# Moving half of a K slot to the front of the load queue, ahead of two weight matrices

## The chip, the cores and the metric

The kernel runs on one core of one Trainium2 chip. The metric is device time in microseconds (us), the median of several executions. The profile's span is some 1.4 us shorter than the device time of the same execution, so spans are compared with spans and times with times.

## The reference

Two decode attention blocks with one query token each, A and B, are computed and their outputs joined. Both have 32 query heads, 16 key/value heads of 128, and a cache of 8192 positions. A looks only at the last 2048 of them, B at all.

```python
q = (x @ wq).reshape(B, Sq, 32, 128)              # x: 1 x 576, wq: 576 x 4096
scores = einsum("bhqd,bhkd->bhqk", q, k) * 128 ** -0.5
o = einsum("bhqk,bhkd->bhqd", softmax(scores), v)
out = o.reshape(B, Sq, 4096) @ wo                 # wo: 4096 x 576
# A: k, v = the last 2048 positions of the cache;  B: all 8192
return concatenate([a, b], axis=-1)
```

Almost all of the work is to read the caches and weights once: 102.76 MB.

## The kernel before

One large tensor, `slots`, holds 4 x 16,384 elements per partition. Slots 0 and 1 take K, slots 2 and 3 take V. Five rounds go through it: round 0 for A, rounds 1 to 4 for B. At the start, parts of it lend their place to the two query weights, `wq`:

```python
SLOT, WQ_W = 16384, 18432
...
WQ = [(4 * SLOT - WQ_W, [("v", 2)]),                           # A's wq: end of the V slots
      (SLOT, [("k", 1, 0), ("k", 1, 1), ("v", 0)])]            # B's wq: K slot 1 and a little of V
for P in range(2):
    off, res = WQ[P]
    x_columns(P)
    load(slots[:, off:off + WQ_W], ... wqs[P] ..., res, "wq%d" % P)   # 128 runs of 36 KB
    q_part(P, off, res)                                        # 36 products that read this wq
    q_finish(P)
...
for g in range(NG):
    for s in range(2):
        load_k(g, s)
    load_v(g)
    ...
```

All these loads are issued by SyncE, in program order, on one queue that the 16 transfer engines serve. A helper derives the waits from `reads` and `writes`: a load waits until the last reader of its place is done. So the load of K slot 1 for A (issued in line 411 of the kernel before) waits for the 36 products on B's wq. A's two K slots are loaded in halves of 2 MB:

```python
for m1 in range(2):                                            # in load_k, for g == 0
    i = 8 * m1 + s
    src = ks[0][0, i:i + 7:2, SK - W_A:, :].rearrange("h (p t) d -> p h (t d)", t=64)
    ins = sp.dma_start(dst[:, m1 * 2 * UNIT:(m1 + 1) * 2 * UNIT], src)   # 128 runs of 16 KB
```

The very first load of the program is issued ahead of the block's opening barrier. The loads are thus issued in this order: A's wq, B's wq, two halves of A's K slot 0, (wait), two halves of A's K slot 1, V.

## Time and profile before

| | before |
|---|---|
| device time, median of 3 | 245.37 us (245.37 to 245.59) |
| span of the profile | 244.0 us |
| bytes read | 102.76 MB |
| share of 16 engines' span taken by the main queue | 98.3% |
| busiest compute engine (TensorE) | 68% |

The kernel is bound by transfers; what counts is any time in which the transfer engines have nothing to do. In the view of busy time by stretch, the columns are the stretch and its length, the five compute engines, TensorE's granted clock, the mean share of the transfer engines in use, and GB/s.

```profile
33.00:34.50 1.50, 0.00 (x0) 0.00 (x0) 0.00 (x0) 0.00 (x0) 0.00 (x0) 0.50 0.95 404
34.50:44.00 9.50, 9.31 (x131) 8.11 (x132) 6.16 (x6) 6.85 (x7) 0.00 (x0) 0.83 1.01 429
```

The engines pass from slot 0 to slot 1 with 0.95 of them in use (transfers are counted by their starts, so values swing a little around 1).

### The profile page before, as it was taken

How to read it: one execution, taken by the hardware profiler on the slowest of the kernel's cores; microseconds unless marked ns; L12 is line 12 of the kernel's file. 1: busy time of each engine (PE TensorE's matmuls, PEld its weight loads, DVE VectorE, ACT ScalarE, POOL GpSimd, SP SyncE). 2: the span in 40 equal slices, each digit the busy share in tenths (PEclk: the TensorE clock that was granted, in tenths of full speed). 3: DMA queues.
4: the chain of work that ended last, by engine and by line, in shares of the span. 5: the costliest groups of instructions: out<-in, count | busy, mean ns of one | idle time of the engine just before them, and what ended most of it. 6: DMA issues, size and time to landing. Idle time of an engine off the chain costs nothing. (4 is left out here: it accounts for less than half of the span.)

```text
span 244.0 us, 5212 instructions
## 1 busy us (share of the span) xinstructions
PE 165.8 (68%) x2325; PEld 120.5 (49%) x2325; DVE 88.2 (36%) x152; ACT 93.2 (38%) x96; POOL 6.4 (3%) x33
## 2 busy tenths in 40 slices
PE   0007539958397997394999473999446699845964
PEld 0002238745237775243978231987332687535753
DVE  0001218855304555203465322456322165533030
ACT  2000018845303876301687500678600387630000
POOL 5000100000000000000000000000000000000000
PEclk9999959997867999657699959799958799965799
DMA  9999999999999999899999999999989999989994
GB/s 344 429 405 422 435 432 422 427 424 427 459 432 426 489 397 462 371 430 435 483 410 451 403 403 435 435 494 408 473 365 440 430 494 397 473 380 417 426 405 172
DMA packets 4064, 102.88 MB, mean 422 GB/s; under 512 B 596, under 2 KB 728, under 8 KB 984
## 3 DMA queue, kind: packets, MB, share of 16 engines
q1 hardware_dynamic: 3896, 102.76, 98.3%
q8 instruction: 6, 0.10, 0.2%
q10 hardware_dynamic: 160, 0.00, 0.0%
q14 instruction: 2, 0.02, 0.0%
HBM read 102.76 MB, written 0.00 MB: 421 GB/s over the span
## 5 line engine op out<-in xcount | busy, mean ns | idle before, releaser
L506 ACT ACTIVATE kt<-ktps 128x1024 bf16<-128x1024 bf16 x80 | 79.8, 1040 | 87.3 <-PE ktps L496 87.2
L496 PE MATMUL ktps<-ident,slots 128*128 128x128 bf16 x1280 | 87.9, 234 | 22.6 <-PEq L214 19.6
L496 PEld LDWEIGHTS ktps<-ident,slots 128*128 128x128 bf16 x1280 | 81.7, 106 | 38.5 <-issue 38.5
L509 DVE COPY kt<-ktps 128x1024 bf16<-128x1024 bf16 x80 | 60.7, 774 | 59.6 <-PE ktps L496 59.6
L588 PE MATMUL opsum<-slots,ptm 128*32 128x512 bf16 x320 | 27.4, 515 | 7.7 <-PEq L214 7.7
L521 PE MATMUL sacc<-kt,qst 128*32 128x512 bf16 x320 | 25.8, 398 | 2.3 <-PEq L214 2.3
L588 PEld LDWEIGHTS opsum<-slots,ptm 128*32 128x32 bf16 x320 | 13.3, 125 | 20.3 <-issue 18.0
L559 PE MATMUL misc<-ident,psb 128*128 128x128 bf16 x40 | 4.3, 271 | 15.8 <-PEq L214 15.8
L547 ACT ACTIVATE psb<-sacc,stat 128x2048 bf16<-128x2048 f32 x5 | 9.8, 1967 | 9.8 <-DVE stat L536 9.8
L606 DVE TENSOR_TENSOR vtmp<-opsum,maskV 128x512 f32<-128x512 f32 x4 | 2.8, 691 | 27.7 <-PE opsum L588 27.7
L438 PE MATMUL misc<-xnine,twice 64*128 64x18 bf16 x1 | 0.2, 170 | 17.8 <-DMA xnine<-in_B_x_dram 17.8
L559 PEld LDWEIGHTS misc<-ident,psb 128*128 128x128 bf16 x40 | 3.1, 118 | 18.3 <-issue 18.3
L521 PEld LDWEIGHTS sacc<-kt,qst 128*32 128x32 bf16 x320 | 5.0, 94 | 8.4 <-issue 4.9
L566 DVE TENSOR_TENSOR ptm<-misc,maskP 128x1024 bf16<-128x1024 bf16 x5 | 3.5, 692 | 15.6 <-PE misc L559 15.6
L438 PEld LDWEIGHTS misc<-xnine,twice 64*128 64x128 bf16 x1 | 0.1, 99 | 17.8 <-issue 17.8
L703 ACT ACTIVATE outsb<-ktps 64x144 bf16<-64x144 f32 x1 | 0.3, 288 | 21.1 <-PE ktps L691 21.1
L691 PE MATMUL ktps<-slots,opj 128*32 128x144 bf16 (+1 forms) x192 | 6.8, 247 | 2.2 <-DMA slots<-in_B_wo_dram 2.2
L462 ACT ACTIVATE qrow<-opsum 128x512 bf16<-128x512 f32 x1 | 0.6, 597 | 19.2 <-PE opsum L456 19.2
L691 PEld LDWEIGHTS ktps<-slots,opj 128*32 128x32 bf16 x192 | 5.2, 97 | 3.6 <-DMA slots<-in_B_wo_dram 3.0
L447 DVE TENSOR_SCALAR xpad<-misc,par 128x5 bf16<-128x5 f32 (+1 forms) x8 | 1.2, 228 | 13.6 <-PE misc L438 13.6
L481 POOL COPY qst<-qcol 128x32 bf16<-128x32 bf16 x8 | 1.7, 213 | 147.5 <-PE sacc L521 147.5
L559 PE MATMUL turned<-ident,psb 128*128 128x128 bf16 x40 | 5.3, 314 | 0.0
(76 smaller groups left out, 57.9 us busy)
## 6 DMA issues: line engine op xcount, KB each, us to landing
slots<-in_B_k_cache_dram SPq DMA_DIRECT2D x8, 4096.0 KB
slots<-in_A_k_cache_dram SPq DMA_DIRECT2D x4, 2048.0 KB
slots<-in_A_v_cache_dram SPq DMA_DIRECT2D x4, 2048.0 KB
slots<-in_A_wq_dram SPq DMA_DIRECT2D x1, 4608.0 KB, 13.9
slots<-in_B_wq_dram SPq DMA_DIRECT2D x1, 4608.0 KB, 24.0
slots<-in_A_wo_dram SPq DMA_DIRECT2D x1, 4608.0 KB, 19.8
slots<-in_B_wo_dram SPq DMA_DIRECT2D x1, 3024.0 KB, 26.6
slots<-in_B_wo_dram SPq DMA_DIRECT2D x1, 1008.0 KB, 9.2
```

Source lines behind the costliest of these rows:

```text
L447: add("dve", lambda dve, dst=dst, o=320 + 9 * P + i, n=n, e=e: dve.tensor_scalar(dst, misc[:, o:o + n], par2[:, e:e + 1], None, ALU.mult), ...
L481: return pool.tensor_copy(dst, src)
L496: ins = pe.matmul(ktps_bf[q][:, t * 128:(t + 1) * 128], lhsT=slots[:, o:o + 128], rhs=ident[:, :], start=True, stop=True, is_transpose=True)
L506: add("act", lambda act, src=src, dst=dst: act.activation(dst, src, ACT.Copy), reads=[("bank", q)], writes=[("kt", u % NKT, q)], tag="e%d% ...
L509: add("dve", lambda dve, src=src, dst=dst: dve.tensor_copy(dst, src), reads=[("bank", q)], writes=[("kt", u % NKT, q)], tag="e%d%d" % (u, q))
L521: ins = pe.matmul(sacc[32 * j:32 * j + 32, :], lhsT=qst[:, o:o + 32], rhs=rhs, start=(u == 0 and e == 0), stop=True, skip_group_check=True)
L547: return act.activation(dst, src, ACT.Exp, bias=st(C_NB + g), scale=SCALE, accum_out=st(C_L + g))
L559: ins = pe.matmul(dst[:, t * 128:(t + 1) * 128], lhsT=psb[:, o:o + 128], rhs=ident[:, :], start=True, stop=True, is_transpose=True)
L566: return dve.tensor_tensor(ptm[:, c * 1024:(c + 1) * 1024].rearrange("p (t y) -> p t y", t=8), dst.rearrange("p (t y) -> p t y", t=8), mas ...
L588: ins = pe.matmul(opsum[64 * j + 32 * x:64 * j + 32 * x + 32, :], lhsT=ptm[:, o:o + 32], rhs=v[:, at[0], at[1], :, :, b:b + 128], start=(n ...
L606: add("dve", lambda dve: dve.tensor_tensor(vtmp[:, :, :], src, by, ALU.mult), reads=[B_O, w], writes=["vtmp"], tag="keep")
L691: ins = pe.matmul(ktps[P + j // 2][32 * j:32 * j + 32, 0:w], lhsT=opj[:, P, at:at + 32], rhs=slots[:, o:o + w], start=(jj == 0), stop=(jj ...
```

## The change

The intent: let the very first transfer be one of short runs (16 KB in place of 36 KB). No byte is added; the first half of A's K slot 0 is taken out of its place behind both wq and put ahead of them.

```diff
-            for m1 in range(2):
-                i = 8 * m1 + s
-                src = ks[0][0, i:i + 7:2, SK - W_A:, :].rearrange("h (p t) d -> p h (t d)", t=64)
-                ins = sp.dma_start(dst[:, m1 * 2 * UNIT:(m1 + 1) * 2 * UNIT], src)
-                if m1 == 0:
-                    op.also.append((32, ins))
-            return ins
-        op = add("sp", go, writes=KS[s], dma="k%d" % s, inc=64)
+            if s == 0:
+                return half_of_A(sp, s, 1)
+            op.also.append((32, half_of_A(sp, s, 0)))
+            return half_of_A(sp, s, 1)
+        op = add("sp", go, writes=KS[s], dma="k%d" % s, inc=64 if g or s else 32)
+
+    def half_of_A(sp, s, m1):
+        ... the load of one half, as above ...
@@
     WQ = [...]
+
+    add("sp", lambda sp: half_of_A(sp, 0, 0), writes=["first"], dma="k0", inc=32)
     for P in range(2):
```

More of the change, by code (lines that the diff above doesn't have):

```diff
@@ L407, in go @@
                 return sp.dma_start(dst, ks[1][0, i:i + 3:2, :, :].rearrange("e (p t) d -> p e (t d)", t=128))
-            for m1 in range(2):
-                i = 8 * m1 + s
-                src = ks[0][0, i:i + 7:2, SK - W_A:, :].rearrange("h (p t) d -> p h (t d)", t=64)
-                ins = sp.dma_start(dst[:, m1 * 2 * UNIT:(m1 + 1) * 2 * UNIT], src)
-                if m1 == 0:
-                    op.also.append((32, ins))
-            return ins
-        op = add("sp", go, writes=KS[s], dma="k%d" % s, inc=64)
+            if s == 0:
[4 more added lines that the diff above has]
+    def half_of_A(sp, s, m1):
+        i = 8 * m1 + s
+        src = ks[0][0, i:i + 7:2, SK - W_A:, :].rearrange("h (p t) d -> p h (t d)", t=64)
+        return sp.dma_start(slots[:, koff(s) + m1 * 2 * UNIT:koff(s) + (m1 + 1) * 2 * UNIT], src)
     def load_v(g):
```

## The prediction

> **What bounds the kernel now.** I began with the page's rows over time and its queue table, to see which resource has no gaps.
>
> ```profile
> PE 165.8 (68%) x2325; PEld 120.5 (49%) x2325; DVE 88.2 (36%) x152; ACT 93.2 (38%) x96; POOL 6.4 (3%) x33
> ...
> DMA  9999999999999999899999999999989999989994
> GB/s 344 429 405 422 435 432 422 427 424 427 459 432 426 489 397 462 371 430 435 483 410 451 403 403 435 435 494 408 473 365 440 430 494 397 473 380 417 426 405 172
> ...
> q1 hardware_dynamic: 3896, 102.76, 98.3%
> ```
>
> No compute engine is above 68%. The transfer engines are at 9 tenths nearly everywhere, and SyncE's queue (q1) keeps all sixteen occupied for 98.3% of the span. Only the first slice (344 GB/s) and the last (172) are low. So time can be won or lost only where the queue stands empty: before the first byte, after the last, or in a hole in between.
>
> The chain that ended last, in order of time, agrees: it ends in a wait for the last weight transfer and a short tail of products and output.
>
> ```profile
> 231.52 0.33 SPq L398
> 231.85 0.04 issue
> 231.89 9.93 DMA slots<-in_B_wo_dram
> 241.82 0.04 issue
> 241.87 0.64 PE ktps L691 x16
> ```
>
> Then I asked for busy time by stretch, for the start, where the change lies. The last two columns are the mean share of the transfer engines in use and GB/s.
>
> ```profile
> 0.00:1.00 1.00, 0.00 (x0) 0.00 (x0) 0.00 (x0) 0.00 (x0) 0.41 (x6) 1.00 0.00 0
> 1.00:3.00 2.00, 0.00 (x0) 0.00 (x0) 0.00 (x0) 0.99 (x1) 2.00 (x8) 1.00 1.13 313
> 3.00:6.00 3.00, 0.00 (x0) 0.00 (x0) 0.46 (x2) 0.50 (x2) 1.19 (x6) 1.00 0.97 418
> 6.00:14.00 8.00, 0.00 (x0) 0.00 (x0) 0.00 (x0) 0.00 (x0) 0.00 (x0) 1.00 1.01 433
> ```
>
> One microsecond passes before any byte. The trace's records of single packets (one packet is one contiguous run) say more: the first packet of an engine starts at 1.04 to 1.5 us (one engine at 2.3), and takes a median of about 2.2 us, where every later 36 KB packet takes 1.364 us. So each engine pays about 0.85 us once for a cold start. That 0.85 us is all that a different first packet could save, since the microsecond before it comes from issuing at all.
>
> The timeline of the issuing queue and of the first weight products gives the dependences of the start:
>
> ```profile
> 0.00 0.41 SPq L398 DMA_DIRECT2D slots<-in_A_wq_dram  x1
> 0.80 0.35 SPq L398 DMA_DIRECT2D slots<-in_B_wq_dram  x1
> ...
> 17.84 0.17 PE L438 MATMUL misc<-xnine,twice 64*128 64x18 bf16 x1 [17.84 <-DMA xnine<-in_B_x_dram]
> ...
> 18.82 4.03 PE L456 MATMUL opsum<-slots,xpad 128*32 128x512 bf16 x36 [0.81 <-DVE xpad L447]
> ...
> 24.80 3.40 PE L456 MATMUL turned<-slots,xpad 128*32 128x512 bf16 x36 [0.99 <-DMA slots<-in_B_wq_dram]
> ```
>
> A narrower window of the same view shows the issue of A's second K slot,
>
> ```profile
> 28.24 1.20 SPq L411 DMA_DIRECT2D slots<-in_A_k_cache_dram  x2
> ```
>
> and the waits of the issuing queue name what holds it up:
>
> ```profile
> SPq L411 <- PE turned L456: 25.7, 1, 25.7
> ```
>
> B's wq lies in the second K slot, so A's second K slot may be issued only when the 36 products that read B's wq are done (28.2 us). Until then the transfer engines live on what was queued before, ending with A's first K slot. By the packet records, the sixteen engines finish that slot between 33.0 and 34.1 us. The queue thus has 33.0 - 28.2 = 4.8 us of **reserve**, less about 1.05 us from issue to first byte. That is the number to watch.
>
> **What the Trainium skill says.** "DMA: Bandwidth & Descriptors", section "Where 436 GB/s comes from", puts the ceiling of 16 ports at 435.2 GB/s. The trace agrees: 16 x 36,864 bytes / 1.364 us = 432 GB/s, and 428 GB/s for 16 KB packets (0.612 us). Run length is therefore worth 1% and the change alters no run's length, only the order. The same page, "Queues, rings and completion order", says that each engine serves its queues in turn, packet by packet. The trace agrees: x, 18-byte packets on ScalarE's queue, passes between packets of wq one at a time and lands 11.4 and 16.4 us after issue. "Perfetto Trace Analysis", "DMA Instruction — HWDGE (DVE, Sync)", says that the slice of a transfer instruction does not contain its data movement; here a slice of 0.41 us stands for a wq that lands after 13.9 us, so I time transfers by packets and by waits. "TensorE: Matmul & The Clock Gate", Part 1, says that the array runs at half clock after an idle window of about 3.4 us and needs as much sustained work to speed up. The trace agrees: the first 36 products advance four per 0.43 us throughout (4.03 us), while the second 36, begun only 0.99 us after other work, speed up in their last groups (3.40 us).
>
> **The change part by part.** Bytes, packets and instruction kinds stay; the instruction order shows one of the four half-slot loads moved ahead of both wq, and nothing else.
>
> (a) *First packets of 16 KB in place of 36 KB.* If the 0.85 us is the latency of a first read that nothing hides, it does not depend on size and nothing is won. If part of it grows with the packet, at most 0.85 us is. I take a gain of 0.2 us.
>
> (b) *x lands earlier.* Its ten small packets per engine pass some 0.6 us apart between 16 KB packets and 1.37 us apart between 36 KB ones. About three packets of the main queue go first and five of the rounds fall among 16 KB packets: roughly 1.05 + 0.85 + 3 x 0.61 + 5 x 0.61 + 5 x 1.37 = 13.6 us, estimated, some 4 us before now. But the products that use it also need A's wq, which (c) delays. Worth 0.
>
> (c) *Both wq land later*, by eight packets of 16 KB per engine: 8 x 0.618 = 4.9 us. A's wq, which I put at 13.9 us now, comes at 18.8; its products start at 18.8 anyway, held by x. No loss. B's wq is waited for until 24.80 now; it comes at 24.80 + 4.9 = 29.7 us.
>
> (d) *The products on B's wq* end 3.40 us later if they run as now, at 33.1. But TensorE will then have idled from about 24 to 29.7 us, so I expect them cold as the first 36 are: up to 4.03 us, ending at 33.8. In the middle, 33.5.
>
> (e) *A's second K slot* is issued then, at about 33.5 in place of 28.2, and its first byte comes 1.05 us or a little more after: 34.6. The bytes ahead of it are the same as before, so the sixteen engines still run dry between 33.0 and 34.1, average 33.6. The reserve is gone and a **hole** of 34.6 - 33.6 = 1.0 us opens (0.5 at the lower end of (d), 1.5 at the upper). A first packet after idling should again pay its cold start, up to 0.85 us. Together about 1.8 us per engine. The engine that ends last is perhaps a late one, which waits less in the hole since all restart together: I take off 0.4.
>
> (f) *After the hole* nothing of it is won back, since the queue is full to the end. The transposes of the first slot start at about 34.9 in place of 34.65, and VectorE's small mask work moves from 29.3 to about 35 us, delaying its first copy (36.6 now) by some 0.4 us. The next load that waits for these is issued at 44.9 us with all of A's second K slot and V queued ahead, so that is hidden.
>
> Sum: -0.2 (a) + 1.8 (e) - 0.4 = +1.2 us; 245.37 + 1.2 gives about **246.5 us**.
>
> **The rivals.** *First: a quicker start and no hole.* If the small first packets save the full 0.85 us and the products run as quickly as now, the hole remains at 0.5 us or so with some restart cost, and gain and loss cancel: 244.9 to 245.4. For it: the first slice is the only low one at the start, and the change is plainly aimed at it. Against it: the cold start does not look like a matter of bytes, and the reserve of 4.8 us is eaten by exactly the 4.9 us of the moved half. *Second: the hole at full size*, cold products, slow issue, restart cost paid in full by the last engine: 1.5 + 0.85 = 2.35, so 247.7 us. For it: the 4.03 us of the cold first products. *Third: everything is hidden*, that is, the engines have more queued than I think, and the time stays at 245.4. Against it: the waits show no other transfer between A's first and second K slots; the half that was moved to the front is the very one that used to cover the wait. *Fourth: the half-slot as first transfer is slow*, its runs lying at power-of-two distances with all engines in step. A tenth more on 4.9 us is 0.5. Against it: the same loads now run at the ordinary 0.612 us.
>
> **Range and chances.** The cases run from about 244.9 to 247.7; I state 245.0 to 247.9 and 246.5 us. Two per cent is 4.9 us, which neither the whole start (2 us) nor the largest hole (2.4 us) reaches: within 2% has 0.98, faster 0.01, slower 0.01.
>
> **What would show it.** In the changed profile: B's wq products should start at 29.5 to 29.8 us and last 3.4 to 4.0; the issue of A's second K slot should come at 33 to 34; the transfer share around 33.5 to 35.5 us should fall clearly below 0.9, with the first packets after it longer than 0.612 us. The wait for x should end near 14 us and the first 36 products start at about 18.8. The first packets' excess over 0.612 us tells (a). The prediction is wrong if there is no hole, or if the start wins more than the hole costs: a time under 245.0.

## The result

The changed kernel takes **246.99 us** (246.78 to 247.11, 6 runs), the kernel before 245.38 us (245.25 to 245.59, 6 runs) in the same rounds: 1.61 us more. The ratio is 1.0063, with a 95% interval of 1.0050 to 1.0076. Ratios here divide the mean of one kernel's runs by the mean of the other's of the same rounds, so they are not quite the ratio of the medians that are quoted.

The page of the changed kernel, rows over time and queue table:

```profile
DMA  7999989999999999999999999999999999999994
GB/s 313 444 451 397 423 345 417 430 427 430 446 425 427 450 470 417 395 438 433 492 402 481 406 395 427 427 460 460 395 406 427 438 470 438 438 397 439 416 406 176
...
q1 hardware_dynamic: 3896, 102.76, 97.7%
```

The first slice fell from 344 to 313 GB/s instead of rising, and the sixth slice (30.7 to 36.8 us), 432 before, shows 345. The timeline around it (issuing queue and TensorE):

```profile
0.00 0.69 SPq L417 DMA_DIRECT2D slots<-in_A_k_cache_dram  x1
...
1.39 0.38 SPq L398 DMA_DIRECT2D slots<-in_A_wq_dram  x1
...
17.32 0.17 PE L440 MATMUL misc<-xnine,twice 64*128 64x18 bf16 x1 [17.32 <-DMA xnine<-in_B_x_dram]
...
18.67 4.02 PE L458 MATMUL opsum<-slots,xpad 128*32 128x512 bf16 x36 [1.18 <-DMA slots<-in_A_wq_dram]
...
29.55 3.70 PE L458 MATMUL turned<-slots,xpad 128*32 128x512 bf16 x36 [5.90 <-DMA slots<-in_B_wq_dram]
```

and a narrower window of it:

```profile
33.30 1.20 SPq L417 DMA_DIRECT2D slots<-in_A_k_cache_dram  x2
```

The first half-slot is issued in 0.69 us where A's wq took 0.41. The products on B's wq begin at 29.55 in place of 24.80 us, and the issue of A's K slot 1 moves from 28.24 to 33.30 us. The same stretch as before, now:

```profile
33.00:34.50 1.50, 0.51 (x12) 0.16 (x4) 0.25 (x2) 0.60 (x1) 0.00 (x0) 1.00 0.26 109
34.50:36.00 1.50, 1.47 (x27) 1.50 (x28) 1.43 (x10) 0.82 (x1) 0.00 (x0) 1.00 0.95 350
```

From 0.95 to 0.26 of the engines in use: this is the hole. By the records of single packets, the engines finish slot 0 by 34.0 us, the first packet of slot 1 starts at 34.63 us, and averaged over 16 engines 1.12 us are idle between 33 and 35 us. On 12 of the 16 engines the first packet after it takes some 0.87 us in place of 0.612, another 0.20 us on average over all. Together this is 1.32 us; the span of this execution is 1.29 us longer than that of the kernel before (245.31 and 244.02 us). (The packet records do not name the engine. Packets are put down to one engine where the start of one follows the end of another.)

### The profile page after: what moved, and what is told of

Same layout as the page of the kernel before. It is cut to its first block, busy times and chain, and to the rows that moved or that the text cites. A ratio compares the mean times of both kernels' runs of the same rounds, so it can differ in the third digit from the quotient of the medians.

```text
span 245.3 us, 5212 instructions
## 1 busy us (share of the span) xinstructions
PE 161.8 (66%) x2325; PEld 115.8 (47%) x2325; DVE 87.8 (36%) x152; ACT 92.7 (38%) x96; POOL 6.3 (3%) x33
## 5 line engine op out<-in xcount | busy, mean ns | idle before, releaser
L498 PE MATMUL ktps<-ident,slots 128*128 128x128 bf16 x1280 | 83.5, 227 | 16.3 <-PEq L214 15.7
L498 PEld LDWEIGHTS ktps<-ident,slots 128*128 128x128 bf16 x1280 | 77.3, 102 | 32.1 <-issue 32.0
L590 PE MATMUL opsum<-slots,ptm 128*32 128x512 bf16 x320 | 28.8, 536 | 14.3 <-PEq L214 14.3
L590 PEld LDWEIGHTS opsum<-slots,ptm 128*32 128x32 bf16 x320 | 14.0, 129 | 27.6 <-issue 25.6
L458 PE MATMUL turned<-slots,xpad 128*32 128x512 bf16 x36 | 3.7, 590 | 5.9 <-DMA slots<-in_B_wq_dram 5.9
L473 DVE CAST qcol<-misc 128x32 bf16<-128x32 f32 x2 | 0.6, 300 | 15.4 <-PE misc L469 15.4
## 6 DMA issues: line engine op xcount, KB each, us to landing
slots<-in_B_wq_dram SPq DMA_DIRECT2D x1, 4608.0 KB, 27.7
```

The source lines that it names most:

```text
L458: ins = pe.matmul((turned if P else opsum)[32 * j:32 * j + 32, :], lhsT=xpad[:, P, u, :], rhs=slots[:, o:o + 512], start=(u == 0), stop=(u ...
L498: ins = pe.matmul(ktps_bf[q][:, t * 128:(t + 1) * 128], lhsT=slots[:, o:o + 128], rhs=ident[:, :], start=True, stop=True, is_transpose=True)
L590: ins = pe.matmul(opsum[64 * j + 32 * x:64 * j + 32 * x + 32, :], lhsT=ptm[:, o:o + 32], rhs=v[:, at[0], at[1], :, :, b:b + 128], start=(n ...
```

## The experiments

Theory: **the hole** makes the whole loss. The issue of K slot 1 hangs on the products on B's wq; whatever delays those beyond the reserve empties the queue. Rival: **the start**, that is, the first transfer itself is costlier (longer issue, later first byte, irregular first packets). Each experiment's "before" is the kernel before in the same rounds (245.36 to 245.52 us).

**1. The same delay, the old start** (`e1_half_between_wq`). The half-slot goes between the two wq.

```diff
-    add("sp", lambda sp: half_of_A(sp, 0, 0), writes=["first"], dma="k0", inc=32)
     for P in range(2):
         ...
         load(... wq of P ...)
+        if P == 0:
+            add("sp", lambda sp: half_of_A(sp, 0, 0), writes=["first"], dma="k0", inc=32)
```

> The moved half of the K slot goes between the two wq, so the first transfer is A's wq in runs of 36 KB as in the kernel before, but B's wq still lands 4.9 us later. Theory of the hole (the issue of A's second K slot waits for the products on B's wq, and the queue runs dry): the hole stays, transfer share far below 0.9 between 33 and 35 us, time 246.7 to 247.2. Rival of the start (the loss comes from the first transfer itself, whose first byte comes 0.35 us later and whose early packets are irregular): the start is that of before, time 245.3 to 245.6.

Measured: 247.03 us (before 245.52; ratio 1.0055, 1.0038 to 1.0072). With A's wq first and the old start, the loss is all there:

```profile
33.00:34.50 1.50, 0.79 (x11) 0.09 (x4) 0.00 (x0) 0.60 (x1) 0.00 (x0) 0.85 0.26 109
```

By the packet records, hole and restart make 1.57 + 0.35 = 1.92 us in this execution, and its span is 1.87 us longer than that of the kernel before. The rival, as the cause of the 1.6 us, falls.

**2. The new start, no delay of B's wq** (`e2_wq_swapped`). `for P in range(2)` becomes `for P in (1, 0)`: B's wq is loaded and used before A's.

> The changed kernel with B's wq loaded and used before A's wq. First transfer as in the changed kernel. B's wq lands at about 18.7 us, its products end near 23, so A's second K slot is issued some 10 us before the queue runs dry. Theory of the hole: no hole, time 245.2 to 245.6. Rival of the start: the start is that of the changed kernel, time 246.8 to 247.1.

Measured: 245.68 us (before 245.52; ratio 1.0007, 0.9990 to 1.0024). K slot 1 is issued at 22.06 us, and there is no hole:

```profile
33.00:34.50 1.50, 0.76 (x12) 0.20 (x5) 0.00 (x0) 0.60 (x1) 0.00 (x0) 0.50 1.18 502
```

So the new start costs nothing that shows, and wins nothing either.

**3. Twice the dose** (`e3_whole_slot_first`). Both halves of K slot 0 go first.

```diff
     add("sp", lambda sp: half_of_A(sp, 0, 0), writes=["first"], dma="k0", inc=32)
+    add("sp", lambda sp: half_of_A(sp, 0, 1), writes=KS[0], dma="k0", inc=32)
```

(and `load_k(0, 0)` is left out of the loop).

> Both halves of A's first K slot ahead of both wq. First packets as in the changed kernel, B's wq another 4.9 us later, with nothing queued behind it. Theory of the hole: the whole 4.9 us adds to the hole, which grows from about 1.1 to about 6 us; time 246.99 + 4.9 = 251.9 (251.3 to 252.4). Rival of the start: as the changed kernel, 247.0.

Measured: 251.94 us (before 245.52; ratio 1.0252, 1.0235 to 1.0269). This is 6.42 us above the kernel before, where the changed kernel is 1.61 us above it: 4.8 us more, nearly as much as the eight further 16 KB packets per engine take (8 x 0.612 = 4.9 us). The queue is empty almost throughout this stretch:

```profile
32.50:39.00 6.50, 4.03 (x36) 1.24 (x36) 0.00 (x0) 0.60 (x1) 0.00 (x0) 1.00 0.01 6
```

By the packet records, the mean idle time grew from 1.12 to 6.2 us. Past the reserve, what is moved ahead is lost one for one.

**4. Same order of loads, dependence cut** (`e4_wq_moved`). B's wq is put 12,288 elements further on, so that it covers only the last quarter of K slot 1 (and more of V), and the lower half of that slot is loaded without a wait.

```diff
-    WQ = [(4 * SLOT - WQ_W, [("v", 2)]), (SLOT, [("k", 1, 0), ("k", 1, 1), ("v", 0)])]
+    WQ = [(4 * SLOT - WQ_W, [("v", 2)]), (4 * SLOT - 2 * WQ_W, [("k", 1, 1), ("v", 0), ("v", 1)])]
...
+        if g == 0 and s == 1:
+            add("sp", lambda sp: half_of_A(sp, 1, 0), writes=["first1"], dma="k1", inc=32)
```

> The changed kernel with B's wq placed 12,288 elements further on in the slots, so that it covers only the upper part of A's second K slot; the lower half of that slot is loaded without a wait. Order of all transfers unchanged. Theory of the hole: the reserve is again 4.9 us more, no hole, time 245.2 to 245.6. Rival of the start: 246.8 to 247.1.

Measured: 245.59 us (before 245.52; ratio 0.9999, 0.9982 to 1.0015). The wait for the products on B's wq still ends late (the second half of slot 1 is issued at 33.76 us), but 2 MB are queued ahead of it, and the hole is gone:

```profile
33.00:34.50 1.50, 0.79 (x11) 0.09 (x4) 0.00 (x0) 0.60 (x1) 0.00 (x0) 1.00 0.97 415
```

Together, experiments 1 to 4 show the cause: the loss stays without the new start (1), goes with the new start when slot 1 is issued in time (2 and 4), and grows with the hole (3). Neither 2 nor 4 beats the kernel before.

**5. Half the dose** (`e5_quarter_first`), and the same once more (`e12_quarter_again`). The first quarter of K slot 0, in runs of 8 KB, goes first; the second quarter and the other half keep the place behind both wq.

```diff
-    add("sp", lambda sp: half_of_A(sp, 0, 0), writes=["first"], dma="k0", inc=32)
+    add("sp", lambda sp: quarter_of_A(sp, 0), writes=["first"], dma="k0", inc=16)
```

> Only a quarter of the K slot (8 packets of 8 KB per engine, about 2.45 us) goes ahead of both wq. B's wq should then be waited for until about 27.1 us, its products end at 30.5 to 30.8, the second K slot's first byte come near 32.0, while the engines have work until 33.4 or later. Theory of the hole, with a threshold at about 3.5 us of moved transfers: no hole, time 245.3 to 245.7. A loss in proportion to what is moved would give half of the change's: 246.2.

> The quarter first once more, on this chip's rounds. On the edge of the hole the runs should scatter more than the other kernels do (0.3 us), between about 245.7 and 246.8, as they did; a fixed cost would give 246.5 each time. A profile with a hole between 33 and 35 us in it would settle what the slower runs hold.

Measured: 246.54 us (245.79 to 246.74; before 245.36) and 246.87 us (246.65 to 247.65; before 245.52). I had expected 245.3 to 245.7 and missed; the repeat lies mostly above the 245.7 to 246.8 that I expected of it. No hole shows at 33 us in either profile, and yet the time is up. In the second profile:

```profile
33.00:34.50 1.50, 0.27 (x4) 0.19 (x4) 1.07 (x5) 0.00 (x0) 0.00 (x0) 0.50 0.97 393
```

The packet records of the second show another gap, early: the 8 KB packets are all done by 4.70 us, but on four engines the first packet of A's wq starts only between 5.5 and 5.8 us. Four engines then end B's wq at 27.7 to 27.9 us, when most others end it near 26.8. In the kernel before, each engine carries 16 of the 256 wq packets, so a late engine is not relieved by the others, and a mean over sixteen hides this. Of the 1.42 us by which this span is longer than that of the kernel before, 0.74 us are added idle time before 6 us and 0.59 us added idle time in the last 14 us of the queue, where the engines run out less evenly (3.56 us idle on average against 2.97).

**6. A quarter of the dose** (`e9_eighth_first`): as the last, with runs of 4 KB.

> An eighth of the K slot (8 packets of 4 KB per engine, 1.2 us) ahead of both wq. In the quarter's profile the second K slot was issued at 31.9 us, later than expected, and its first bytes had only some 0.2 to 0.5 us to spare, with no hole, while the unprofiled runs were 1.2 us slower than the kernel before. If the quarter sits on the edge of the hole, moving half as much restores about 1.2 us of reserve: no hole, 245.3 to 245.8. If the loss of the quarter comes from short packets in front: 246.2 to 246.8 here too.

Measured: 247.70 us (before 245.52; ratio 1.0093, 1.0076 to 1.0110): of the half, the quarter and the eighth, the eighth is the slowest. This speaks against my reading of experiment 5 as the edge of the hole and for the early gap. From 1 to 3 and 3 to 4.5 us this kernel moves

```profile
1.00:3.00 2.00, 0.00 (x0) 0.00 (x0) 0.00 (x0) 0.51 (x1) 1.73 (x8) 1.00 0.72 213
3.00:4.50 1.50, 0.00 (x0) 0.00 (x0) 0.00 (x0) 0.97 (x2) 1.27 (x5) 1.00 1.08 336
```

where the kernel before has 313 (its line stands in the prediction) and 393 GB/s:

```profile
3.00:4.50 1.50, 0.00 (x0) 0.00 (x0) 0.46 (x2) 0.50 (x2) 1.19 (x6) 1.00 0.91 393
```

Two engines end B's wq at 27.5 us, the others between 25.7 and 26.7. A small hole is there as well: three of the sixteen engines run dry at 34.3 us. By the packet records, the 2.36 us of longer span are 0.94 us of idle time before 6 us, 0.30 us between 33 and 44 us, 0.41 us of longer packet times and 0.70 us at the end.

**7. The quarter with the dependence cut** (`e11_quarter_wq_moved`): experiment 5 with the placement of experiment 4.

> The quarter first, together with the moved place of B's wq, so that half of the second K slot is issued without a wait. If the quarter's loss of 1.2 us is a hole at its edge: 245.3 to 245.7. If it is the start with 8 KB runs: 246.3 to 246.8.

Measured: 246.09 us (245.61 to 246.56; before 245.52; ratio 1.0030, 1.0010 to 1.0050), between the two expectations, with a wide scatter. With 2 MB queued ahead of the late wait, part of the loss remains, and one engine again ends B's wq at 27.36 us, the next at 27.05. So the start with 8 KB runs seems to cost something by itself. Whether all of the quarter's loss comes from it stays open.

**8. A shorter first packet, nothing moved** (`e6_wq_half_first`, `e7_wq_eighth_first`). The kernel before with A's wq cut into two transfers, the first with 18 KB or 4.5 KB runs.

```diff
+    cut = 9216        # 2304 in the second kernel
+    add("sp", lambda sp: sp.dma_start(slots[:, WQ[0][0]:WQ[0][0] + cut], src(0)[:, 0:cut]), writes=["first"], dma="wq0", inc=16)
+    load(slots[:, off + cut:off + WQ_W], lambda: src(0)[:, cut:], res, "wq0")
```

> The kernel before with A's wq cut into two transfers of 18 KB runs, no other order. It asks whether a shorter first packet has a cheaper cold start when the first transfer is still issued as quickly (first byte at 1.05 us). If the cold start shrinks with the packet as it did in the changed kernel (0.85 us to 0.2 to 0.4) and is kept to the end: 244.8 to 245.1. If it is not kept: as before, 245.4.

> As the last, but the first transfer is an eighth of A's wq, in runs of 4.5 KB. If what counts is the size of the first packet: 244.6 to 245.0. If the short packets come one at a time with gaps: 245.4 or a little more.

Measured: 245.30 and 245.33 us (before 245.36; ratios 0.9996 and 0.9999, both intervals within 0.2% of 1). The first packets are indeed shorter (a median of 1.25 and 0.47 us against 2.17), but little of that is kept: by 5 us packets of 1.16 and 1.11 MB have ended, against 1.11 MB before (1.34, 1.38 and 1.28 MB if packets still under way are counted by their share). I had expected up to 0.8 us from the second kernel and missed. The aim of the change, a better start through shorter runs, wins nothing here that shows; the intervals would still hide 0.4 us.

**9. Faster products on B's wq** (`e8_busy_before_wq`, then `e10_busy_fewer`). TensorE is kept busy with useless products between its two uses of wq, so that it does not come to the second one from an idle stretch. First 72 products of 128 columns, then 25 of 512 (shown).

```diff
         x_columns(P)
+        if P == 1:
+            def busy(pe):
+                for _ in range(25):
+                    ins = pe.matmul(ktps[0][:, :], lhsT=ident[:, :], rhs=slots[:, WQ[0][0]:WQ[0][0] + 512], start=True, stop=True)
+                return ins
+            add("pe", busy, reads=["ident", ("v", 2)], writes=[("bank", 0)])
```

> The changed kernel, with 72 products of the identity with itself put on TensorE between its two uses of wq, into a bank that is not in use yet. They keep TensorE busy from about 23.7 to 29.5 us, so the 36 products on B's wq should run at full clock: about 1.9 to 2.2 us in place of 3.70. The second K slot is then issued 1.5 to 1.8 us earlier and its first byte comes near 33.0. Theory of the hole, its length set by the products: the hole all but vanishes, time 245.4 to 245.8. If the hole were not the cause: 247.0.

Measured: 248.28 us (before 245.36; ratio 1.0122, 1.0107 to 1.0138), which I had not expected. The useless products ended at 27.77 us, yet those on B's wq began only at 31.00 us and ran at 3.45 us. K slot 1 was issued at

```profile
34.50 1.20 SPq L417 DMA_DIRECT2D slots<-in_A_k_cache_dram  x2
```

which is 1.20 us later than in the changed kernel, and the loss against the kernel before is 1.3 us larger. That the later issue lengthens the run is again the theory. Why the products began late is shown in part: an instruction fetch of 16 KB now stood at 28.87 to 29.78 us in the packet records, where the changed kernel has its first at 38.80 us, and the last of the sixteen 4-byte completion packets of B's wq came only at 29.76 us, the others by 29.23. The 1.2 us from there to 31.00 us stay open.

> The test of the busy TensorE again, with 25 products of 512 columns in place of 72 of 128, since the 144 extra instructions had moved an instruction fetch of TensorE to 28.9 us, into the landing of B's wq. Fewer instructions should leave that fetch after 33 us. Products on B's wq then start at about 29.5 us at full clock and take 1.9 to 2.3 us; the second K slot is issued near 31.7 and its first bytes come near 33.0. Theory of the hole: no hole, time 245.4 to 245.8; anything that delays the products again moves the time by the same amount.

Measured: 246.53 us (246.01 to 246.76; before 245.52; ratio 1.0048). The products took 2.13 us in place of 3.70, slot 1 was issued at 31.65 us, and the hole closed:

```profile
29.47 2.13 PE L458 MATMUL turned<-slots,xpad 128*32 128x512 bf16 x36 [0.89 <-DMA slots<-in_B_wq_dram]
...
31.65 1.20 SPq L417 DMA_DIRECT2D slots<-in_A_k_cache_dram  x2
...
33.00:34.50 1.50, 0.00 (x0) 0.00 (x0) 1.43 (x11) 0.00 (x0) 0.00 (x0) 1.00 1.04 415
```

but the time came back by less than half a microsecond of the expected 1.2 to 1.6, to 246.0 in the profiled execution and 246.5 to 246.8 in the others. So the theory missed here. By the packet records the engines idle for 0.01 us on average between 33 and 36 us, with next to no time to spare, and yet the span is 0.53 us longer than that of the kernel before: 0.45 us more idle time lies in the last 14 us of the queue, where the engines run out less evenly. Why is open. Whether the executions that weren't profiled have a small hole at 33 us, or lose elsewhere, stays open too.

## Why the prediction was right

It said 246.5 us, 245.0 to 247.9, within 2%; measured 246.99. By its steps:

- **(a) first packets.** Right in part. The cold start did shrink with the packet, from 0.85 to about 0.27 us (median first packet 0.88 us against 0.612). But the microsecond before it, which I took as given, grew: the half-slot takes 0.69 us to issue, and the sixteen first packets start at 1.54 us on average in place of 1.24. And the seven packets that follow on each engine take 0.638 us in place of 0.612, together 0.18 us. This leaves 0.58 - 0.30 - 0.18 = 0.1 us of gain. Experiments 2, 4 and 8 show no gain, but their intervals would not exclude the 0.2 us that I took.
- **(b) x lands earlier.** Wrong in size: the wait for x ends at 17.32 us, not near 14. The first of x's small packets started at 5.57 us, when most of the half-slot had already passed, so only a few of its ten rounds fell among short packets. Nothing hung on it, as said.
- **(c) both wq later.** Right. The products on A's wq start at 18.67 us (said 18.8), now held by wq and not by x; those on B's wq at 29.55 (said 29.7).
- **(d) the products.** Right: 3.70 us, within 3.4 to 4.03 (29.7 + 4.03 is 33.7, not the 33.8 that stands there). Where in this range they fell was luck, since the idle time before them does not settle it: after the same 5.90 us of idle they took 4.03 us in experiment 4, and the first 36 products of the program, which also follow a long idle stretch, took 3.41 us in the repeat of experiment 5. What experiment 9 shows is that they get much faster, 2.13 us, right after 5.55 us of other products.
- **(e) the hole.** Right in mechanism and nearly in size. Issue at 33.30 us (said 33.5); idle 1.12 us on average (said 1.0). One reading was off: in the kernel before, the first engine finishes slot 0 at 33.4 us and not at 33.0, so the reserve was 5.1 us and not 4.8; but the average of 33.6 us, on which the hole was worked out, is right. The restart was mis-sized: 0.20 us on average and not up to 0.85, which was taken from 36 KB packets; the first 16 KB packets of the program too took only 0.27 us longer than later ones. Hole and restart make 1.32 us, not 1.8.
- **The deduction of 0.4 us** because all engines restart together did not show: hole and restart, 1.32 us, account for the whole 1.29 us of the profiled execution. It is luck that the sum came so near: the restart taken too large and this deduction nearly cancelled. The profiled execution was the fastest of six; where the others lose a further 0.2 to 0.3 us is open.
- **(f)** Right: nothing is won back. The transposes begin at 34.53 us, VectorE's first copy at 36.58, unchanged and not 0.4 us later.

Of the rivals, the second (hole at full size, 247.7) is excluded by the range of the runs, the first (a quicker start that saves the full 0.85 us and pays for the hole) by the time and by experiments 2, 4 and 8, the third (all hidden) by the profile. The fourth, a half-slot that is slow as the first transfer, finds no support in 2 and 4.

## What to carry to other kernels

In a kernel bound by transfers, count the reserve before reordering the queue: the time for which work is queued behind the point at which the next issue waits, less the delay from issue to first byte. Moving a transfer that covered such a wait to another place spends the reserve although no byte is added, and past it the loss is one for one. And here the first transfer needed enough bytes to last until the next one's first byte on every engine: with 8 KB runs in front, four engines of sixteen stood idle until 5.5 us or later, and the end of the run became less even. So look at single packets, not only at means.

## What the Trainium skill lacked or had wrong

- "DMA: Bandwidth & Descriptors", section "Latency and other measured facts", gives about 600 ns to the first byte for transfers issued from SyncE. From the start of the instruction it was 1.04 us (A's wq first) and 1.41 us (half-slot first), and 1.33 us for K slot 1 (33.30 to 34.63 us). The page roughly agrees only if one counts from the end of the instruction's slice: 1.04 - 0.41 = 0.63, 1.41 - 0.69 = 0.72 and, with a slice of 0.55 us, 34.63 - 33.85 = 0.78 us. It doesn't say from where to count.
- No page gives the cost of a load's access pattern for its issue: 0.41 us for 128 plain rows, 0.69 us for 128 runs spread over four heads, both as the first instruction.
- The section "Queues, rings and completion order" of the same page describes turns by packet, but not how late a second queue gets its first turn: x was issued at 0.80 us (before) and 1.39 us (after), and its first packet started at 5.26 and 5.57 us.
- No page gives the restart of an emptied queue: most first 16 KB packets took 0.87 us after the hole against 0.612 otherwise.
